# One load ahead of four crossbar transposes, a score tile for the last rows of x, and full-array steps in front of the AV runs, in a fused attention and GELU kernel

## The chip, the cores and the metric

One core of one Trainium2 chip. The metric is the device time of one execution in microseconds (us). The kernel before takes 350.77 us (median of three runs, 350.18 to 350.9). Granted TensorE clocks are given as shares of full speed. A run is called slow when it is over 1.5% above the fastest of the same kernel; ratios use the other runs, the fast ones. A kernel counts as faster or slower from 2% on; no verdict here reaches that (part 3 alone is once "unclear", all others are "same"), so the arguments rest on the traces. Three chips served for the experiments, and each experiment is compared with runs of the kernel before on its own chip.

## The reference, cut to what matters

Causal attention with a forget gate for 8 batches x 8 heads x 576 tokens x 64, then a two-layer GELU network on the 4608 rows that come out.

```python
q, k, v: (8, 8, 576, 64)   f: (8, 8, 576)   w_in: (512, 2048)   w_out: (2048, 512)
cum    = cumsum(log(clip(f, 1e-4, 1)))
scores = q @ k.T / 8 + cum[:, :, :, None] - cum[:, :, None, :]     # causal
x      = softmax(scores) @ v                                       # -> (4608, 512)
out    = gelu(x @ w_in) @ w_out
```

## The kernel before: the parts that matter

The kernel works batch by batch. In a batch, TensorE makes the scores of four head pairs, each in four tiles; ScalarE takes the exponentials; GpSimd masks the diagonal blocks; TensorE multiplies with v (an "AV run": two heads, 30 products); VectorE normalizes the rows, which are transposed into xT. Then the first product (`gemm1`, 16 blocks of 4 products with w_in) runs alone. The second product of the previous batch fills the gaps of the attention, a few steps at a time.

q and k of batch b come in through GpSimd's queue, which also turns them to bf16, are transposed by the crossbar from SyncE's queue, and are untangled by VectorE during the first product of batch b-1. v comes in on SyncE's queue too, and GpSimd multiplies it with the forget weights ("weighs" it). v has one buffer, so its load waits for the weighing of the batch before. Batch 1 has a layout of its own:

```python
def load_v(b, h0=0, h1=H):                    # five loads on SyncE's queue
    for n in range(NBLK):
        nc.sync.dma_start(v_sb[...], v[b, ...])

def transpose_dma(b, h0, h1):                 # one q and one k transpose, SyncE's queue
    for src, dst in zip(qk_of[b], tq_of[b]):
        nc.sync.dma_start_transpose(dst[...], src[...])

def untangle(b, i):                           # VectorE: 4 copies for q, 4 for k (L242)
    ...
def weigh_v(b, i, eng=nc.gpsimd):             # L258: vw = v * w, a head pair at a time
    ...
def second_attention():                       # batch 1
    ...
    for i in range(HP):
        for t in range(4):
            scores(b, i, t)
            ...
            if (i, t) == (3, 0):
                transpose_dma(2, 0, 4)
                transpose_dma(2, 4, 8)
    ...
    gemm1_begin(1, both)
    x_tail(1)
    load_v(2)                                 # behind the transposes

for b in range(B):
    ...
    for ffb in range(0 if b > 1 else 4, n_ff):
        gemm1(b, ffb)                         # 16 blocks; 12 of them for batch 1
        ...
        if b == 1 and ffb == 4:
            load_qk_tokens(3)                 # GpSimd's queue; q,k have two buffers
        first, gap = (5, 3) if b == 1 else (0, 4)
        at, late = divmod(ffb - first, gap)
        if late == 0:
            untangle(b + 1, at)
        if late == gap - 2:
            weigh_v(b + 1, at)
        if ffb == 14 and b > 1:
            load_qk_tokens(b + 2)
```

The second product takes row steps ("r": two products on 64 rows each, side by side into two PSUM banks) or full-array steps ("n": one product on 128 rows into one bank):

```python
PLAN = [                                      # block of rows, banks, steps
    (0, "o", 16 * "r"),
    (1, "m", 15 * "r" + "n"),
    (2, "m", 16 * "r"),
    (3, "s", 8 * "r" + 8 * "n"),
]
```

PSUM has two banks each under the names "o" (AV results) and "m" (products), and two double tiles "s" (scores). The transpose of x through TensorE takes an "o" bank.

The softmax here doesn't subtract the row's maximum and nothing guards it: scores larger than these inputs give would overflow.

## Time and profile before

| | before |
|---|---|
| time, median of 3 | 350.77 us |
| profiled span | 348.6 us, TensorE busy 96% |
| first AV run of batch 2, with the full step ahead of it | 84.26 to 87.00 us |
| the next AV run, with its step | 90.97 to 92.30 us |
| first crossbar-transposed k of batch 2 copied from | 62.94 us |
| length of a batch from batch 3 on | 36.3 us |

The instants are read from the timelines of single engines, in us from the start of the profiled span: a line there gives start, length, engine, source line, operation, operands, count, and in brackets the idle time just before it with what ended it. The lines themselves stand in the prediction.

### The profile page before, as it was taken

To read this page: it belongs to the slowest core of one execution; us is meant where nothing else is said; L and a number is where in the kernel's file an instruction comes from. 1 tells how busy PE (TensorE), PEld (TensorE's weight loads), DVE (VectorE), ACT (ScalarE), POOL (GpSimd) and SP (SyncE) were. 2 spreads that over 40 slices of the span, in tenths; PEclk is the share of its full clock that TensorE was granted. 3 is DMA by queue.
4 is the path that set the end of the run, shared out by engine and by line. 5 is a ranking of instruction groups with operands and counts; after the bars stand their busy time and mean duration, and the time that the engine had idled before them with its cause. 6 is when DMAs were issued, how large, how long until landed. Compare 5 with 4: busy or idle time off the path is not lost.

```text
span 348.6 us, 7941 instructions
## 1 busy us (share of the span) xinstructions
PE 334.8 (96%) x3211; PEld 175.9 (50%) x3242; DVE 188.0 (54%) x424; ACT 212.8 (61%) x296; POOL 124.0 (36%) x256
## 2 busy tenths in 40 slices
PE   8899999998989999999999999999999999999995
PEld 3674555444554455545654465446544554444443
DVE  4770456853366934796469746975498452011011
ACT  5976786772643687468746874687567764603600
POOL 8480872109328034443436243714270430000000
PEclk9999999999999999999999999999999999999999
DMA  7999999992990999268944997398900130011013
GB/s 117 177 190 194 196 197 193 174 188 80 215 199 30 137 187 185 83 87 159 202 121 73 132 233 139 55 159 199 176 32 0 52 100 30 2 60 60 2 30 91
DMA packets 99924, 43.03 MB, mean 123 GB/s; under 512 B 78704, under 2 KB 95344, under 8 KB 99888
## 3 DMA queue, kind: packets, MB, share of 16 engines
q1 hardware_dynamic: 82592, 28.37, 41.1%
q0 software_dynamic: 16896, 13.63, 26.3%
q8 instruction: 25, 0.41, 0.5%
q10 hardware_dynamic: 400, 0.52, 0.4%
q14 instruction: 11, 0.09, 0.1%
HBM read 36.85 MB, written 9.44 MB: 133 GB/s over the span
## 4 chain that ended last, share of the span: by engine, by line
PE 68%; DMA 10%; SPq 10%; ACT 4%; POOL 4%; issue 2%; DVE 0%; POOLq 0%; ACTq 0%; DVEq 0%
PE ps L370 28%; PE ps L461 20%; PE ps L403 8%; PE o L318 7%; SPq L117 7%; DMA v_sb<-in_v_dram 6%; PE s L287 5%; DMA k<-in_k_dram 3%; SPq L228 3%; POOL vw L258 2%; ACT e L297 2%; ACT L297 2%; ACT g L387 1%; PE ps_x L348 1%; POOL q L105 1%
## 5 line engine op out<-in xcount | busy, mean ns | idle before, releaser
L387 ACT ACTIVATE g<-ps 128x512 bf16<-128x512 f32 x144 | 85.3, 597 | 81.8 <-PE ps L370 81.8
L297 ACT ACTIVATE e<-s 128x896 bf16<-128x896 f32 (+2 forms) x128 | 101.6, 837 | 32.6 <-PE s L287 30.9
L370 PE MATMUL ps<-xT,w_in_sb 128*128 128x512 bf16 x502 | 111.6, 379 | 0.5
L461 PE MATMUL ps<-w_out_sb,g 64*128 64x512 bf16 (+1 forms) x756 | 102.7, 376 | 1.1 <-issue 0.8
L370 PEld LDWEIGHTS <-w_in_sb 128*128 128x128 bf16 x576 | 55.9, 98 | 67.5 <-issue 1.8
L299 POOL TENSOR_SCALAR_AFFINE_SELECT e<-e 128x256 bf16<-128x256 bf16 (+1 forms) x135 | 49.2, 383 | 101.4 <-ACT e L297 101.1
L461 PEld LDWEIGHTS <-g 64*128 64x128 bf16 (+1 forms) x771 | 41.7, 94 | 36.2 <-issue 5.5
L242 DVE COPY qT<-tq 64x288 bf16<-64x288 bf16 x96 | 49.1, 511 | 1.7 <-DMA tq<-q 0.3
L287 PE MATMUL s<-qT,kT 64*128 64x320 bf16 (+4 forms) x384 | 46.0, 277 | 4.0 <-ACT e L297 2.6
L258 POOL TENSOR_TENSOR vw<-v_sb,wT 128x640 bf16<-128x640 f32 x31 | 39.7, 1281 | 22.3 <-DMA v_sb<-in_v_dram 22.2
L318 PE MATMUL o<-vw,e 128*128 128x65 bf16 x960 | 37.5, 194 | 2.7 <-issue 0.8
L469 DVE COPY ot<-ps 128x512 f32<-128x512 f32 x26 | 17.9, 690 | 40.7 <-PE ps L461 36.5
L318 PEld LDWEIGHTS <-e 128*128 128x128 bf16 x960 | 33.6, 98 | 12.1 <-issue 7.3
L242 DVE COPY kT<-tk 64x288 bf16<-64x288 bf16 x96 | 32.6, 340 | 2.8 <-DMA tk<-k 1.2
L332 DVE TENSOR_TENSOR x<-o,r 128x320 bf16<-128x320 f32 x64 | 31.5, 492 | 2.4 <-DVE r L331 0.2
L287 PEld LDWEIGHTS <-kT 64*128 64x128 bf16 x384 | 20.2, 94 | 24.8 <-issue 11.7
L412 DVE COPY ot<-ps 128x512 f32<-128x512 f32 (+2 forms) x9 | 5.7, 633 | 48.8 <-PE ps L403 48.8
L403 PE MATMUL ps<-w_out_sb,g 128*128 128x512 bf16 (+2 forms) x142 | 27.9, 355 | 0.1
L331 DVE RECIPROCAL r<-o 128x5 f32<-128x5 f32 x64 | 12.2, 190 | 27.6 <-PE o L318 27.4
L403 PEld LDWEIGHTS <-g 128*128 128x128 bf16 x144 | 13.5, 98 | 14.5
L471 DVE TENSOR_TENSOR ot<-ot,ps 128x512 f32<-128x512 f32 x26 | 17.9, 688 | 1.5
L360 POOL COPY tails<-xT 128x256 bf16<-128x256 bf16 x8 | 3.2, 396 | 31.9 <-DVE xT L351 31.9
(64 smaller groups left out, 160.1 us busy)
## 6 DMA issues: line engine op xcount, KB each, us to landing
out_dram<-ot SPq DMA_DIRECT2D x32, 256.0 KB, 2.3
v_sb<-in_v_dram SPq DMA_DIRECT2D x24, 256.0 KB, 4.9
q<-in_q_dram POOLq DMA_DIRECT2D x6, 576.0 KB, 6.3
k<-in_k_dram POOLq DMA_DIRECT2D x6, 576.0 KB, 8.5
v_sb<-in_v_dram SPq DMA_DIRECT2D x22, 128.0 KB, 5.6
w_in_sb<-in_moe_w_in_dram POOLq DMA_DIRECT2D x4, 512.0 KB, 6.8
w_out_sb<-in_moe_w_out_dram POOLq DMA_DIRECT2D x4, 512.0 KB, 11.9
q<-in_q_dram POOLq DMA_DIRECT2D x4, 144.0 KB, 4.5
```

What stands on the lines that cost most here:

```text
L117: nc.sync.dma_start(v_sb[p0:P, h0:h1, n, :], v[b, h0:h1, K0[n] + p0 : K0[n] + P].rearrange("h p d -> p h d"),)
L242: nc.vector.tensor_copy(rows[:, odd], src[odd * D : (odd + 1) * D, 2 * i + h].rearrange("d j p -> d p j"),)
L258: eng.tensor_tensor(vw_of[b][:, hs, :, 0:D], v_sb[:, hs, :, :], w.unsqueeze(3).to_broadcast([P, 2, NBLK, D]), Alu.mult,)
L287: nc.tensor.matmul(to, *ab, start=half < 0, stop=half == 1 or not masked)
L297: nc.scalar.activation(et[:, :, z:c], st[:, :, z:c], Act.Exp, scale=scale)
L299: nc.gpsimd.affine_select(out=et[:, :, c0 + z : c0 + P], in_=et[:, :, c0 + z : c0 + P], compare_op=Alu.is_ge, fill=0.0, base=z, pattern=[[ ...
L318: nc.tensor.matmul(o[:, m, :], e_of[b, i, t][:, h, c : c + P], vw_of[b][:, 2 * i + h, n, :], start=(n == 0), stop=(n == m),)
L332: nc.vector.tensor_tensor(x_of[b, i][:, :, h, :], o[:, :, 0:D], r.unsqueeze(2).to_broadcast([P, NBLK, D]), Alu.mult,)
L370: nc.tensor.matmul(ps, w_in_sb[:, kt, ffb * P : (ffb + 1) * P], src[:, kt, 0:TC], start=(kt == 0), stop=(kt == n_dm - 1),)
L387: nc.scalar.activation(g_of[c][ffb], ps, Act.Gelu)
L403: nc.tensor.matmul(pss[ts][:, c0:c1], g_of[c][kt][:, ts * P : (ts + 1) * P], w_out_sb[:, kt, c0:c1], start=(kt == 0), stop=(kt == n_ff - 1),)
L461: nc.tensor.matmul(banks[r], g_of[c][kt][rows, ts * P : (ts + 1) * P], w_out_sb[rows, kt, :], start=(kt == 0), stop=last if r else kt == n ...
```

## The change

The intent was to take away three small idle times of TensorE. (1) Wherever an AV run follows row steps, a full-array step is put between them, since a switch from half-array to full-array products costs a little time. (2) The transpose of the last rows of x but one in batch 2 goes through a score tile, so that the last AV run needn't wait for an "o" bank. (3) v of batch 2 is queued ahead of the crossbar transposes of batch 2's q,k, so that it is weighed, and the masks are made, before the first AV run of batch 2 needs them.

```diff
 def to_xT(b, i, copy, pool=m_psum, tag="m", ps=None):
     if ps is None:
-        ps = pool.tile([P, XC], BF16, tag=tag, name="ps_x")
+        shape = [P, 2, 1024] if pool is s_psum else [P, XC]
+        ps = pool.tile(shape, BF16, tag=tag, name="ps_x")
+        if pool is s_psum:
+            ps = ps[:, 0, 0:XC]
 ...
 PLAN = [
     (0, "o", 16 * "r"),
-    (1, "m", 15 * "r" + "n"),
-    (2, "m", 16 * "r"),
-    (3, "s", 8 * "r" + 8 * "n"),
+    (1, "m", 5 * "r" + "n" + 9 * "r" + "n"),
+    (2, "m", 9 * "r" + "n" + 6 * "r"),
+    (3, "s", 7 * "r" + 9 * "n"),
 ]
 ...
 if b == 2:
-    to_xT(b, HP - 2, nc.vector.tensor_copy, o_psum, "o")
+    to_xT(b, HP - 2, nc.vector.tensor_copy, s_psum, "s")
 ...
+if (i, t) == (2, 0):
+    load_v(2)
 if (i, t) == (3, 0):
     transpose_dma(2, 0, 4)
     transpose_dma(2, 4, 8)
 ...
 x_tail(1)
-load_v(2)
```

## The prediction

> **What bounds the kernel now.** I read the page first, then the chain of waits, then the timelines of the engines where the chain leaves TensorE.
>
> ```profile
> span 348.6 us, 7941 instructions
> PE 334.8 (96%) x3211; PEld 175.9 (50%) x3242; DVE 188.0 (54%) x424; ACT 212.8 (61%) x296; POOL 124.0 (36%) x256
> ```
>
> TensorE is busy 334.8 of 348.6 us and no other engine is over 61%. A change can only pay where it fills TensorE's 13.8 us of idle time or shortens the stream itself. The chain of waits (start, length, what) leaves TensorE for long between 41 and 86 us:
>
> ```profile
> 41.52 12.04 DMA k<-in_k_dram
> 53.57 4.04 SPq L228
> 57.66 2.72 SPq L228
> 60.43 2.31 SPq L228
> ...
> 66.38 12.21 DMA v_sb<-in_v_dram
> 78.75 1.28 POOL vw L258
> ...
> 84.33 1.66 POOL e L299 x5
> 86.04 0.97 PE o L318 x25
> ```
>
> So: q,k of batch 2 land, SyncE issues their four crossbar transposes (L228), then the load of v; v lands at 78.6 us; GpSimd weighs it (L258), and only then masks the exponentials (L299) that the first AV run of batch 2 (the products with v, L318) waits for. TensorE's timeline shows what that costs, against the next AV run, which waits for nothing:
>
> ```profile
> 84.26 0.38 PE L461 MATMUL ps<-w_out_sb,g 128*128 128x512 bf16 x1 [0.16 <-issue]
> 84.72 0.23 PE L318 MATMUL o<-vw,e 128*128 128x65 bf16 x2
> 85.68 1.32 PE L318 MATMUL o<-vw,e 128*128 128x65 bf16 x28 [0.73 <-POOL e L299]
> ...
> 90.97 0.38 PE L461 MATMUL ps<-w_out_sb,g 128*128 128x512 bf16 x1 [0.16 <-issue]
> 91.19 1.11 PE L318 MATMUL o<-vw,e 128*128 128x65 bf16 x30
> ...
> 101.70 0.64 PE L318 MATMUL o<-vw,e 128*128 128x65 bf16 x15
> 103.03 0.64 PE L318 MATMUL o<-vw,e 128*128 128x65 bf16 x15 [0.69 <-DVE xT L351]
> ```
>
> The first run takes 84.26 to 87.00 (85.68+1.32), that is 2.74 us; the second 90.97 to 92.30, 1.33 us. Loss: 1.41 us. The last run is cut in two, because its second head needs the o bank that the transpose of x just filled and VectorE has not emptied: 103.03 - 101.70 = 1.33 us from head to head where about 0.46 (half a run's pace) is enough. Loss: about 0.87 us.
>
> VectorE then shows how batch 2's q,k are unpacked (L242, "untangled") during the first product of batch 1:
>
> ```profile
> 60.40 1.34 DVE L242 COPY qT<-tq 64x288 bf16<-64x288 bf16 x4 [0.32 <-DMA tq<-q]
> 62.94 1.36 DVE L242 COPY kT<-tk 64x288 bf16<-64x288 bf16 x4 [1.20 <-DMA tk<-k]
> ...
> 71.76 1.34 DVE L242 COPY kT<-tk 64x288 bf16<-64x288 bf16 x4
> 74.77 0.69 DVE L507 TENSOR_TENSOR ot<-ot,ps 128x512 f32<-128x512 f32 x1 [1.67 <-PE ps L496]
> ```
>
> The first transposed q landed at about 60.4, the first k at 62.9, and the eight groups of four copies (q and k of four head pairs) end at 73.1. TensorE's scores of batch 2 start at 72.53. This slack is what the change spends.
>
> **What the Trainium skill says.** "DMA: Bandwidth & Descriptors", section "Queues, rings and completion order": each DMA engine takes turns between the queue rows that have work, a packet at a time, and descriptors of one row are consumed in ring order. The packet records agree: from 68 to 74 us, with q,k of batch 3 (packets of 768 B, GpSimd's queue) beside v (256 B, SyncE's queue), both move about 180 to 200 packets per us; v alone at 86 to 90 moves about 950 per us, the transposes alone at 94 to 98 about 800. So a GpSimd load cuts the SyncE queue to a quarter. "TensorEngine Tiling (Array Packing)", section "Key Properties": "Mode switching requires drain". The trace agrees, and it is cheap: about 0.12 us per switch, below. "TensorE: Matmul & The Clock Gate", section on the array's architectural detail: VectorE's queue is strictly first in, first out; so the two additions of L507 cannot pass untangling copies that are issued before them. In this trace they never do.
>
> **The change, part by part.**
> 1. *Full-array step in front of AV.* A step is either two 64-row products into two banks, side by side, or one 128-row product. Both cost about 0.216 us from start to start. In the steady batches of before, one AV run already has the full step in front, and the others don't:
>
> ```profile
> 163.22 1.04 PE L461 MATMUL ps<-w_out_sb,g 64*128 64x512 bf16 x8
> 164.20 1.12 PE L318 MATMUL o<-vw,e 128*128 128x65 bf16 x30
> ...
> 167.44 0.82 PE L461 MATMUL ps<-w_out_sb,g 64*128 64x512 bf16 x6
> 168.43 1.11 PE L318 MATMUL o<-vw,e 128*128 128x65 bf16 x30 [0.16 <-issue]
> ```
>
> Without it: four row steps, 4 x 0.216 = 0.86, from 163.22 give 164.08; AV starts at 164.20, 0.12 late. With it (its record is missing, but its weight load is there): three row steps and one full, also 0.86, from 167.44 give 168.30; AV starts at 168.43, 0.13 late. The drain is paid ahead of the full step instead of ahead of AV. AV itself is 0.01 shorter. Net 0.00 us for each of 3 runs x 5 batches; I allow 0.2 either way.
> 2. *The last rows of x through a score tile.* Removes the 0.87 us wait. But the transpose of the last x (105.00) comes 6 steps later and needs VectorE to have normalized both heads: 103.93+0.49 = 104.42 now, about 104.26 with the second head right behind the first. TensorE would be there at about 104.15, so it starts at about 104.4 instead of 105.0. Gain 0.6 us.
> 3. *v ahead of the transposes.* v's load then waits only for the weighing of batch 1, done at 46.7, so its packets start at about 48 instead of 64. v is weighed and masks are written in time: gain 1.41 us. What it pushes back: v has 4608 packets. Beside q,k and w_out on GpSimd's queue (still about 1040 packets of 768 B at 185 per us and 1024 of 1024 B at 155: 5.6+6.6 us, so to about 60.3), v moves about 2100; the other 2500 at 1000 per us end at about 62.7. The transposes stand behind them in the ring.
> The built program adds something that the diff doesn't show. In before, the pool gives q,k of batch 3 the buffer of batch 2, so that their load waits for the transposes (issued at 64.31, the first q and k transposes long landed). In the changed build they get batch 1's buffer, and wait for TensorE's old reads only. GpSimd can issue them at 60.6; with the 2.5 us to first packets seen in before they run from about 63.0 to 71.5 (1536 at 180). The transposes meet them from the start: some 300 packets alone, 8.5 x 180 = 1530 beside them, then 750 per us. The first q and k need 2304, reached at 72.1; in before landing came 1 to 2 us after the count. So the first k lands at about 73.5, not 62.9.
> From there VectorE has all groups but the first q's to copy, 7 x 1.35 = 9.45, then two L507 of 0.69, with 0.1 of signals: the banks of the second product are free at 73.5+10.9 = 84.4. TensorE wants them at its 49th step after 72.53, at 80.75. Delay 3.7 us: about 2.4 of it before the first scores (73.5+1.45 against 72.53), the rest at that bank.
> Sum: -0.0 -0.6 -1.4 +3.7 = +1.7 us, 352.4.
>
> **The rivals.** (a) The transposes are fast enough: if the first k lands before 80.75-10.95 = 69.8, nothing of the 3.7 is paid and the time is 350.8-2.0 = 348.8. For it: v is finished at about 62, and alone a transpose takes some 1.6 us. Against it: under a GpSimd load the first one needed from 54 to 60.4. (b) Part paid: landing near 71.5 makes 1.7 us of delay and a tie, 350.5. (c) Landing at 75 or later, a long idle of TensorE and perhaps a lower clock after it: 354 or more. The clock row shows no loss after short idles in before. (d) A true gain from part 1, if the weight loads of AV hide behind the full step: at most the 0.01 us per run seen, 0.2 in all.
>
> **Range and chances.** I give the sum with a late transpose 65%, rival (a) 25%, the rest to ties; weighted, 351.3. The range 348.7 to 353.8 holds all but (c). Two per cent is 7.0 us, and no part comes near it: faster 0.01, slower 0.02.
>
> **What would show it.** VectorE's timeline: first kT<-tk copy of batch 2 near 73.5 (theory) or under 69.8 (rival a); the first scores of batch 2 after a wait on VectorE; the first L461 step on the m banks waiting for L507. GpSimd's issue of q for batch 3 near 60.6. The first AV run of batch 2 unbroken, 1.33 us with its full step; the last one unbroken. AV runs of later batches 0.12 us behind a row step, as before; batch length still 36.3 us (164.20 to the next batch's 200.5). If later batches change in length, part 1 is misjudged; if the first k lands early, my packet rates are.

## The result, and the profile after

The changed kernel takes 353.15 us (median of four: 352.74, 352.71, 353.56 and a slow one of 359.14); the kernel before, in the same rounds, 350.75. The ratio is 1.0067 (95%: 1.0045 to 1.0089): a little slower, within 2%. Ratios here are the mean time of one kernel's fast runs over that of the other's fast runs of the same rounds, so not quite the ratio of the medians quoted.

Two lines of the page of the changed kernel:

```profile
span 350.7 us, 7898 instructions
PE 332.4 (95%) x3182; PEld 175.5 (50%) x3227; DVE 187.7 (54%) x424; ACT 212.7 (61%) x296; POOL 124.9 (36%) x256
```

The span is 2.1 us longer. The number of TensorE instructions is no measure of the work here: some matmul records are missing from each trace. The weight loads (PEld), 15 fewer, fit the plan: each of 3 added full steps, in 5 batches, loads one weight tile where a row step loads two.

GpSimd's timeline of the changed kernel: the load of q of batch 3, and the first weighing of v of batch 2.

```profile
60.74 0.84 POOL L105 DMA_DIRECT2D q<-in_q_dram  x1
...
64.47 1.28 POOL L258 TENSOR_TENSOR vw<-v_sb,wT 128x640 bf16<-128x640 f32 x1 [2.12 <-PE ps L373]
```

The load of batch 3's q is issued at 60.74 (64.31 before; 60.6 was predicted), because it no longer waits for the transposes. The weighing begins at 64.47 instead of 78.75. That was what the reordering is for.

The chain of waits of the changed kernel (start, length, what), where it leaves v's load for the transposes:

```profile
58.09 3.26 SPq L117
...
61.39 10.75 DMA tq<-q
```

SyncE finishes issuing v (L117) at 61.35, and the first transpose is issued at 61.39 and lands 10.75 us later, at 72.14. The packet records, counted per microsecond, say why: SyncE's queue moved nothing from 63.81, where v's last packet started, to 66.23, while GpSimd's load moved 250 to 265 packets per us alone; from 67 to 70 the transposes moved 185 to 189 per us, as many as that load (184 to 190); from 70 on, with the load ending (last packet at 71.12), 424 to 1120. The first k landed at 73.09.

VectorE's timeline of the changed kernel from there on:

```profile
72.16 1.34 DVE L242 COPY qT<-tq 64x288 bf16<-64x288 bf16 x4 [12.01 <-DMA tq<-q]
73.52 1.35 DVE L242 COPY kT<-tk 64x288 bf16<-64x288 bf16 x4
...
82.03 1.49 DVE L242 COPY kT<-tk 64x288 bf16<-64x288 bf16 x4
83.55 1.29 DVE L510 TENSOR_TENSOR ot<-ot,ps 128x512 f32<-128x512 f32 x2
```

The eight groups of copies run from 72.16 to 83.52 instead of 60.40 to 73.10. The additions (L510; L507 before) that empty the two "m" banks of the second product stand behind them and end at 84.84.

TensorE's timeline. First three lines of before that the prediction doesn't show: the first scores of batch 2, the first eight products after them, and the first step into the "m" banks.

```profile
72.53 0.37 PE L287 MATMUL s<-qT,kT 64*128 64x256 bf16 x4
72.83 1.90 PE L496 MATMUL ps<-w_out_sb,g 128*128 128x512 bf16 x8
...
80.75 1.89 PE L461 MATMUL ps<-w_out_sb,g 64*128 64x512 bf16 x16
```

The same stretch in the changed kernel, then the first and the last AV run of batch 2, and one AV run of a later batch:

```profile
74.23 0.28 PE L287 MATMUL s<-qT,kT 64*128 64x256 bf16 x1 [1.56 <-DVE kT L242]
74.93 0.36 PE L287 MATMUL s<-qT,kT 64*128 64x256 bf16 x3 [0.41 <-DVE kT L242]
75.22 1.90 PE L499 MATMUL ps<-w_out_sb,g 128*128 128x512 bf16 x8
...
84.29 0.37 PE L464 MATMUL ps<-w_out_sb,g 64*128 64x512 bf16 x1 [0.99 <-DVE ot L510]
84.89 1.88 PE L464 MATMUL ps<-w_out_sb,g 64*128 64x512 bf16 x15 [0.23 <-DVE ot L510]
...
88.39 0.38 PE L464 MATMUL ps<-w_out_sb,g 128*128 128x512 bf16 x1 [0.16 <-issue]
88.61 1.11 PE L318 MATMUL o<-vw,e 128*128 128x65 bf16 x30
...
104.42 1.11 PE L318 MATMUL o<-vw,e 128*128 128x65 bf16 x30
...
165.24 0.82 PE L464 MATMUL ps<-w_out_sb,g 64*128 64x512 bf16 x6
166.22 1.11 PE L318 MATMUL o<-vw,e 128*128 128x65 bf16 x30 [0.16 <-issue]
```

Both AV runs that were broken are now whole, the first at 88.61 and the last at 104.42 (30 products in 1.11 us each). In exchange TensorE waits in two new places: 1.56 + 0.41 us for the untangled k, and 0.99 + 0.23 us for a bank that VectorE empties late. The account, from instants of these two timelines (start to start):

| stretch | before | after | difference |
|---|---|---|---|
| start of the span to the first AV run of all | 17.38 | 17.45 | +0.07 |
| from there to the full step ahead of batch 2's first AV run (84.26; 88.39) | 66.88 | 70.94 | +4.06 |
| from that step to the next AV run's step (90.97; 93.69) | 6.71 | 5.30 | -1.41 |
| from the second AV run (91.19; 93.91) to batch 3's first (127.90; 129.92) | 36.71 | 36.01 | -0.70 |
| sum up to batch 3 | | | +2.02 |
| batches 3 to 6 (to the first AV run of batch 7) | 145.18 | 145.20 | +0.02 |

The +4.06 and the offset of 0.07 make 4.13, and split so: the first scores come 1.70 later (72.53 to 74.23), the eight products after them another 0.69 later, the first step into the banks another 1.15, and from that step to the full step another 0.59.

### The profile page after: what moved, and what is told of

It is laid out like the page before. It is cut to its first block, busy times and chain, and to the rows that moved or that the text cites. A ratio compares the mean times of both kernels' runs of the same rounds, so it can differ in the third digit from the quotient of the medians.

```text
span 350.7 us, 7898 instructions
## 1 busy us (share of the span) xinstructions
PE 332.4 (95%) x3182; PEld 175.5 (50%) x3227; DVE 187.7 (54%) x424; ACT 212.7 (61%) x296; POOL 124.9 (36%) x256
## 4 chain that ended last, share of the span: by engine, by line
PE 67%; SPq 10%; DMA 6%; ACT 5%; DVE 4%; POOL 4%; issue 3%; POOLq 0%; ACTq 0%; DVEq 0%
PE ps L373 28%; PE ps L464 19%; SPq L117 10%; PE ps L406 8%; PE o L318 7%; PE s L287 5%; DMA tq<-q 3%; DMA v_sb<-in_v_dram 3%; ACT e L297 3%; ACT L297 2%; DVE qT L242 2%; POOL vw L258 1%; DVE kT L242 1%; ACT g L390 1%; PE ps_x L351 1%
## 5 line engine op out<-in xcount | busy, mean ns | idle before, releaser
L464 PE MATMUL ps<-w_out_sb,g 64*128 64x512 bf16 (+1 forms) x731 | 100.9, 376 | 2.0 <-DVE ot L510 1.2
L299 POOL TENSOR_SCALAR_AFFINE_SELECT e<-e 128x256 bf16<-128x256 bf16 (+1 forms) x135 | 50.0, 387 | 117.9 <-ACT e L297 117.5
L318 PEld LDWEIGHTS <-e 128*128 128x128 bf16 x960 | 34.8, 98 | 5.3 <-PE ps_x L351 0.3
L474 DVE TENSOR_TENSOR ot<-ot,ps 128x512 f32<-128x512 f32 x26 | 17.9, 687 | 1.5
L373 PE MATMUL ps<-tails,w_in_sb 128*128 128x512 bf16 x63 | 14.3, 377 | 0.1
```

The lines of the kernel that those rows point to most:

```text
L299: nc.gpsimd.affine_select(out=et[:, :, c0 + z : c0 + P], in_=et[:, :, c0 + z : c0 + P], compare_op=Alu.is_ge, fill=0.0, base=z, pattern=[[ ...
L318: nc.tensor.matmul(o[:, m, :], e_of[b, i, t][:, h, c : c + P], vw_of[b][:, 2 * i + h, n, :], start=(n == 0), stop=(n == m),)
L373: nc.tensor.matmul(ps, w_in_sb[:, kt, ffb * P : (ffb + 1) * P], src[:, kt, 0:TC], start=(kt == 0), stop=(kt == n_dm - 1),)
L464: nc.tensor.matmul(banks[r], g_of[c][kt][rows, ts * P : (ts + 1) * P], w_out_sb[rows, kt, :], start=(kt == 0), stop=last if r else kt == n ...
```

## The experiments

**The theory at this point:** parts 1 and 2 do what was predicted; part 3's loss comes from the load of batch 3's q,k, which lost its wait and slows the transposes of batch 2. **Rivals:** v ahead of the transposes is by itself too late for them, whatever the load does; or part 1 costs time, hidden by gains elsewhere.

### Each part alone (one chip; the kernel before there: 350.98, 349.16 to 354.12, 11 runs)

The first kernel has the three lines of `PLAN` alone:

> Before with part 1 alone (full-array step in front of three more AV runs of each of five batches). Theory (a mode switch costs about 0.12 us wherever it falls): same time as before, within 0.2 us, and the batches stay 36.3 us long. Rival (the full step hides the first weight loads of AV, or the switch was dearer in front of AV): 15 runs gain 0.1 us each, 1.5 us faster.

Measured: 351.44 us (349.86 to 354.3), ratio 1.0019 (0.997 to 1.0067). The times can't settle tenths. The trace can: first AV runs of batches 3, 4 and 5 at 128.78, 165.08 and 201.37, so 36.30 a batch, against 36.29 before. Part 1 is worth nothing, and costs nothing: the drain of a switch is paid ahead of the full step instead of ahead of AV.

The second has the edit of `to_xT` and its score tile alone:

> Before with part 2 alone (last rows of x of batch 2 through a score tile). Theory: the last AV run of batch 2 is unbroken and the transpose of the last x starts 0.6 us earlier, total 0.6 us faster. Rival (VectorE's queue sets the second transpose anyway): under 0.2 us.

Measured: 350.13 us (348.77 to 353.03), ratio 0.9985 (0.9935 to 1.0034). In its trace the last AV run of batch 2 is whole, and the second AV run to batch 3's first takes 36.00 us (92.58 to 128.58) instead of 36.71. Part 2 gains 0.71.

The third has the move of `load_v(2)` alone:

> Before with part 3 alone (v of batch 2 ahead of the transposes; its build also gives q,k of batch 3 the buffer of batch 1). Theory: this part alone holds the whole loss: the changed kernel's +2.1 us of span and the 0.6 us that part 2 gives back, so about 2.7 us slower than before, first k copy of batch 2 near 73.5 us, VectorE done with the copies and the two additions near 84.8. Rival (the loss comes from an interplay of the three parts): under 1.5 us slower.

Measured: 357.3 us (354.45 to 358.17), ratio 1.0165 (1.0113 to 1.0216; unclear, since the interval reaches past 2%). A miss by more than 3 us. The trace shows a thing that the changed kernel's doesn't: v's last load landed only at 71.7 instead of 64.2, so v was weighed from 72.02 to 77.86, right beside the first untangling copies. The first q group took 3.61 us instead of 1.34, TensorE sat idle 4.42 us before the first scores, and the eight products after them took 3.56 us instead of 1.90.

### Does part 3 do this only when alone? The changed kernel and part 3 again (a third chip; before there: 352.36, 349.88 to 355.94, 11 runs)

Both kernels unchanged, on one chip. The changed kernel:

> The changed kernel again, beside the others on one chip. Theory: its time is not one number but depends on how long TensorE waits for the first k of batch 2: near 353 where the last load of v got ahead of q,k of batch 3, and 356 to 359 where it did not, because v is then weighed beside the copies and TensorE's wait grows past 4 us and its clock drops. So a spread of over 3 us between runs, with granted clocks of 0.99 in the long ones. Rival (the long run seen at first was chance): all runs within 1 us of 353.

Measured: 356.41 us (355.4 to 357.39, and one run at 352.33), ratio 1.0089 (1.0028 to 1.0151; the kernel before is slower and more spread on this chip). Part 3 alone again:

> Part 3 alone again. Theory: it has the same spread as the changed kernel, plus 0.6 us; on one chip the two differ by 0.6 us or by which of the two cases a run falls in. Rival (parts 1 and 2 protect the changed kernel): part 3 alone always longer by 3 us or more.

Measured: 356.8 us (355.3 to 357.75), ratio 1.0113 (1.006 to 1.0166), and the same pattern in its trace. So it is no property of part 3 alone: the changed kernel has two ways to run. Its trace here, first on GpSimd and VectorE:

```profile
71.65 1.28 POOL L258 TENSOR_TENSOR vw<-v_sb,wT 128x640 bf16<-128x640 f32 x1 [9.37 <-PE ps L373]
...
73.10 4.64 DVE L242 COPY qT<-tq 64x288 bf16<-64x288 bf16 x4 [13.01 <-DMA tq<-q]
```

And on TensorE:

```profile
78.47 0.39 PE L287 MATMUL s<-qT,kT 64*128 64x256 bf16 x1 [5.87 <-DVE kT L242]
...
79.65 3.45 PE L499 MATMUL ps<-w_out_sb,g 128*128 128x512 bf16 x8
```

Compare line by line with the changed kernel's first trace. On GpSimd the weighing starts at 71.65, not 64.47, as v's fifth load landed only at 71.35 (the profile puts the wait down to a product on TensorE, which was long done). The issue of that load ended at 63.02 here and at 61.35 there, while the load of batch 3's q was issued at the same time (60.68 and 60.74). With 1.7 us less of a head start v's last packets fell under GpSimd's load and came out 7 us later: SyncE's queue pauses here too, from 64.56 to 66.52, and only 4096 of v's 4608 packets, four of its five loads, had gone before the pause; in the first trace all 4608 had. Both traces of part 3 alone show the late case (4096 before a pause). That the head start decides is read from these four traces; no run moved it alone. The first copies fall beside the weighing and take 4.64 us. TensorE's idle time before the scores is 5.87 us, and the eight products after it take 3.45 us.

The windows of this trace (stretch, its length, busy time and instructions of TensorE, its weight loads, VectorE, ScalarE and GpSimd, then granted clock, DMA share, GB/s) show why the products are slow:

```profile
79.00:84.00 5.00, 4.83 (x19) 1.63 (x20) 4.76 (x15) 2.73 (x3) 0.85 (x2) 0.62 0.00 0
```

The clock is 0.62 after the idle time; in the changed kernel's first trace, after 1.56 + 0.41 us of idle, the same window has 1.00. The Trainium skill, "TensorE: Matmul & The Clock Gate", section "What's actually happening", gives half clock after an idle window of about 3.4 us. The idle time of 5.87 us agrees: it began at 72.61, and the granted clock was 1.00 up to 76.0 and 0.50 from there to 82.8. That of 4.42 us, in part 3 alone, agrees less well: it began at 74.43, and the clock was 0.50 from 76.6 on, 2.2 us into it. These runs still count as fast, for they are compared with their own fastest run; the mean clock of 0.99 marks them. The slow run of 359.14 in the first result has a clock of 0.99 too, but no trace, so its cause isn't shown.

### Taking the load of batch 3 out of the way

Three experiments take the load away from the transposes. First, the changed kernel with q,k of batch 3 asked for behind the weighing (on the chip of the single parts):

```diff
-if b == 1 and ffb == 4:
-    load_qk_tokens(3)
 ...
-if ffb == 14 and b > 1:
+if ffb == (15 if b == 1 else 14):
     load_qk_tokens(b + 2)
```

> The changed kernel, but q,k of batch 3 are asked for behind the four weighings of batch 2 instead of ahead of them. v still stands ahead of the transposes. Theory (the load of q,k of batch 3 beside the transposes is what delays them): the load goes out near 70 us, the transposes run alone from about 64 us, the first k copy of batch 2 starts near 67.5, before 69.8, no TensorE wait at the first scores; about 348.8 us, 2.0 faster than before and 4.2 faster than the changed kernel. Rival (v ahead in the same ring is enough to delay them): first k near 70 or later and 350.5 or more.

Measured: 350.46 us (349.58 to 352.57), ratio 0.9991 (0.9947 to 1.0035). The first half of the theory holds: without the load beside them SyncE's queue has no pause, and the first q and k landed at 65.92 and 67.57. The gain didn't come, since the copies still ended late, at 81.47 instead of 83.52, and the wait at the bank stayed (0.99 + 0.22 us). The answer for the tile qT (count: shortest, median and longest duration in ns, first and last start, form) and GpSimd's timeline of this kernel:

```profile
L242 DVE COPY qT<-tq x4: 681/1445/1452, 65.9 to 69.6; 64x288 bf16<-64x288 bf16 x4
```

```profile
66.62 1.27 POOL L258 TENSOR_TENSOR vw<-v_sb,wT 128x640 bf16<-128x640 f32 x1
...
68.09 1.27 POOL L258 TENSOR_TENSOR vw<-v_sb,wT 128x640 bf16<-128x640 f32 x1
```

A copy that takes about 0.33 us otherwise takes 1.445, and GpSimd's period is 68.09 - 66.62 = 1.47 us. While GpSimd weighs, VectorE gets one copy through per weighing. The Trainium skill, "SBUF — State Buffer", section "Who interferes with whom", calls the pair of ports that the two engines share an exclusive lock: the engine that comes second is blocked for the whole instruction of the first, not slowed down. The numbers agree.

Second, the changed kernel with fixed buffers, so that q,k of batch 3 go to batch 2's buffer and wait for the transposes, as in the kernel before (on a second chip; before there: 352.12, 349.8 to 354.53, 11 runs):

```diff
-qk_pool = ...tile_pool(name="qk", bufs=2)
+qk_pool = ...tile_pool(name="qk", bufs=1)
-    qk_pool.tile([PT, H, JT * D], BF16, tag=n, name=f"{n}{b}")
+    qk_pool.tile([PT, H, JT * D], BF16, tag=f"{n}{(b + (b > 2)) % 2}", name=f"{n}{b}")
```

> The changed kernel with one thing undone by hand: q,k of batch 3 get the buffer of batch 2 again, as before's build had it, so that their load waits for the transposes; nothing moves in the program. Theory (the lost wait is the cause): the load goes out near 69 us, the first k copy of batch 2 starts near 67.5, no TensorE wait at the first scores, 348.8 us. Rival (v ahead of the transposes is enough): as the changed kernel, 352 or more.

Measured: 355.72 us (353.41 to 356.64), ratio 1.009 (1.0038 to 1.0142). Again the transposes are early (first copies of q and k at 65.96 and 67.50) and the first scores on time (72.56). But the load waits for the transposes on GpSimd, in order, and the weighing stands behind it: 72.14 to 78.10. The third q group beside it took 5.73 us, the copies ended at 82.72, TensorE waited 2.55 us at the bank, and then the clock fell, as the windows of this trace show:

```profile
84.00:87.00 3.00, 2.91 (x14) 1.15 (x15) 1.33 (x3) 0.00 (x0) 0.00 (x0) 0.50 0.86 249
```

Third, what settles whether v ahead of the transposes is too late by itself: the first of these three kernels, with GpSimd's weighing held until VectorE has copied the last k (a tiny GpSimd copy reads it). Run on the third chip:

```diff
-if late == gap - 2:
+if late == gap - 2 and b > 1:
     weigh_v(b + 1, at)
+if b == 1 and ffb == 15:
+    done = x_pool.tile([P, 1], BF16, tag="done", name="done")
+    nc.gpsimd.tensor_copy(done, kT[3][:, S - 1 : S])
+    for pair in range(HP):
+        weigh_v(2, pair)
```

> The changed kernel with q,k of batch 3 asked for late (as in the run before it of that kind), and the four weighings of batch 2 held back until VectorE has copied the last k. Theory (GpSimd's weighing beside the copies was what cost the 4 us there, 5.06 instead of 1.34 for the first group): all eight groups take 1.34 to 1.6, first k copy near 67.5, copies done near 77, the additions near 78.2, no wait at TensorE's bank; v weighed from 77 to 82.5, first AV run of batch 2 waits under 0.5 us; 348.8 to 349.4 us. Rival (v ahead of the transposes is itself too late): copies end after 80, 350.5 or more.

Measured: 352.12 us (351.76 to 353.3), ratio 0.9991 (0.9936 to 1.0046). The total misses, but the point in question is answered on VectorE's timeline:

```profile
68.72 1.36 DVE L242 COPY kT<-tk 64x288 bf16<-64x288 bf16 x4 [0.31 <-DMA tk<-k]
```

All eight groups take 1.34 to 1.36 us, the copies end at 78.29, and TensorE waits for VectorE neither at the first scores nor at the bank. So v ahead of the transposes isn't too late by itself; the load beside the transposes and the weighing beside the copies are what cost. The total misses because the time is only handed on: weighing ends at 84.2, masks at 88.4, and the first AV run of batch 2 is broken again (1.03 + 0.71 us of waits). The profile puts the first of these waits down to an addition of VectorE (L474) that ended at 86.18, but the first mask ended at that time too, and in the changed kernel the run starts before that addition ends (88.61 against 89.76). Later comes a wait of 0.89 us for a transpose of x, on a SyncE queue that runs late: v of batch 3, now beside the late load, lands at 99.11 instead of 92.95.

### The other order

The kernel before, with q,k of batch 3 in batch 1's buffer (the tag becomes `f"{n}{b % 2}"`), so that the load comes early while the transposes still stand ahead of v, on the second chip:

> Before with q,k of batch 3 in batch 1's buffer, so that their load no longer waits for the transposes (it goes out near 60.6 us instead of 64.3); v stays behind the transposes. Theory (the lost wait costs only when the transposes still stand behind v): the first q and k have landed by 63, only the last two transposes meet the load, the copies still end before 80; v lands between 76 and 79, so the first AV run still waits up to 1.4 us; 350.0 to 350.8, as before. Rival (the early load is harmful by itself): over 1.5 us slower than before.

Measured: 349.96 us (349.61 to 350.96), ratio 0.9931 (0.9887 to 0.9976). An early load does no harm there. Its trace is not a clean comparison, with everything up to batch 2 about 1.7 us later than in the trace of before (first scores of batch 2 at 74.22). In batch 0 TensorE waits 0.54 us for k there, and its granted clock is 0.50 from 17.1 to 20.5. Its first AV run of batch 2 is whole, for which that delay may be needed.

Last, a version meant to beat both: the kernel before with part 2, and the load of batch 3 behind the weighing as in the first of the three above. The transposes stay ahead of v. On the second chip:

> Before with part 2, and q,k of batch 3 asked for behind the weighings of batch 2; v stays behind the transposes. If the contention of that load with whatever stands on SyncE's queue is the cause on both sides, v moves alone from 64 us and lands near 70 instead of 78.6, the first AV run of batch 2 is unbroken (gain 1.4), the copies are as in before, part 2 gives 0.6: about 348.8 us without part 3. Rival (v lands late for its place in the ring): the AV wait stays, 350.2.

Measured: 348.68 us (347.88 to 348.97), ratio 0.9887 (0.9843 to 0.9931), as expected. Once more on the third chip:

> Transposes ahead of v, q,k of batch 3 asked for behind the weighings, x through a score tile: a repeat on another chip or at another hour. Theory: 348.7 again, 2 us faster than a before that is not disturbed (350.7), and little spread, since nothing on TensorE's path then depends on a race of two loads. Rival: its lead of 1.1 per cent was due to a slow before, under 0.2 per cent here.

Measured: 348.39 us (348.31 to 349.07), ratio 0.9883 (0.9835 to 0.9932). VectorE and then TensorE in this trace:

```profile
71.20 5.67 DVE L242 COPY kT<-tk 64x288 bf16<-64x288 bf16 x4
```

```profile
84.30 1.11 PE L318 MATMUL o<-vw,e 128*128 128x65 bf16 x30
```

Without the load beside it v lands in time to be weighed from 70.99 on (78.75 before), early enough for the masks and a whole AV run. The weighing still blocks one group (5.67 us), but it is the last, with slack behind it: the two additions end at 78.2, and TensorE takes the banks at 80.58. This is the best version, 2.1 to 2.4 us under an undisturbed run of before (350.75). The larger ratio of 1.2% is partly due to the kernel before, which spreads from 350 to 356 us on those two chips. The granted clocks point to the reason: its ten runs of 353.3 us or more on the three chips show 0.990 to 0.995, the other 23 show 0.997 to 1.0, and the trace with q,k of batch 3 in batch 1's buffer, at 0.994, has one stretch at half clock in batch 0. That the long runs of before have the same isn't shown, for no trace of one was taken.

## Why the prediction was right, and where it was not

The time, 351.3, is the sum of the parts (352.4) weighted with rivals. The result of 353.15 lies in the range, and within 2%. Step by step:

- **Full steps, 0.00: right.** Batches keep 36.30 us, in the changed kernel and in the part alone; AV still starts 0.12 us late, at 166.22, where six row products and the full step from 165.24 make 165.24 + 4 x 0.216 = 166.10.
- **Score tile, -0.6: right**, measured -0.70 in the whole and -0.71 alone.
- **Whole first AV run, -1.41: right**, measured -1.41.
- **The delay, +3.7: right in mechanism, mis-sized by 0.36** (measured 4.06). The term that was off is the copying: seven groups were put at 7 x 1.35 = 9.45, and took 83.52 - 73.52 = 10.00, as three of them needed 1.44 to 1.55. Beside each of these GpSimd wrote masks (from 77.66, 80.61 and 82.25); in the kernel with the held weighing no mask ran beside the copies, and none needed more than 1.36. The banks came free at 84.84 instead of 84.4. The part before the first products was put at 2.4 and measured 75.22 - 72.83 = 2.39.
- **The first k at 73.5: 73.09 landed, 73.52 copied, but by luck, as two errors cancelled.** The transposes did not meet the load "from the start" at 180 packets per us: nothing moved on their queue from 63.8 to 66.2, and up to 1120 per us moved at the end. The first q, which the sum took as copied already when k lands, landed only at 72.14.
- **Rival (a), an early landing: fell.** It came true only where the load was taken away (first k landed at 67.57), and even there the gain was not kept.
- **Rival (c), a long idle and a lower clock, left outside the range: it exists.** It did not decide the first result, but five of six runs of the changed kernel on the third chip took 355.4 to 357.4. The step behind it that failed was the even flow of v: that v ends "at about 62.7" was taken as settled, when it is a race of v's last load with GpSimd's. And the sum didn't know that weighing and untangling exclude each other: from a late v follow late copies, though the transposes land nearly on time (73.10 for the first q copy instead of 72.16).
- **Slips that moved nothing much.** Half an AV run's pace is 0.52 us, not 0.46 (91.19 to the next instruction at 92.23, halved). The row step at 80.75 is the 33rd step after 72.53; it is the 49th product. From GpSimd's issue to its load's first packet before shows 2.0 us (64.31 to 66.28), not 2.5.

So the load that lost its wait was found in the built program ahead of the run, and is about half of the story: with it moved away, the first AV run of batch 2 starts 86.56 - 17.22 = 69.34 us after the first of all, against 88.61 - 17.45 = 71.16 in the changed kernel, and 67.10 would be no delay at all (84.26 + 0.22 for the full step, less 17.38), so 2.24 of the 4.06 remain. What was missed is that v and the transposed q,k meet a second time, as weighing and untangling, on GpSimd and VectorE.

## What to carry to other kernels

Before a load is moved ahead in a queue, work out who is now behind it and what else may start earlier in the built program: here a buffer pool gave the next load another buffer, and with it took a wait away that had kept two transfers apart. Where long pieces of GpSimd and VectorE block each other, as weighing and untangling do here, plan them into different stretches, or let the blocked piece be one with slack behind it. A median near the prediction may be one of two ways to run: run it on another chip and look at the trace before the sum is believed.

## What the Trainium skill lacked or had wrong

- "TensorE: Matmul & The Clock Gate", section "What's actually happening": an idle window of about 3.4 us isn't needed to lose the clock. An idle time of 2.55 us at a bank, one product, and 0.18 us more were followed by a clock of 0.50 for the next 3 us (15 products in 3.36 us instead of 1.88). With q,k of batch 3 in batch 1's buffer, the clock was 0.50 from 17.1 to 20.5 after waits of at most 0.54 us; TensorE had been busy 2.00 of the 3.41 us before, with small products. Idle times of 1.56 + 0.41 us were not followed by it (1.00). Where the line runs, these traces don't say.
- "SBUF — State Buffer", section "Who interferes with whom": right on the lock, but it doesn't say what a run of GpSimd instructions does. VectorE got one copy in for each weighing, 1.445 us a copy instead of 0.33, so that four weighings held one group of four copies for 3.6 to 5.7 us instead of 1.34.
- "DMA: Bandwidth & Descriptors", section "Queues, rings and completion order": taking turns by packet is stated and agrees (185 to 189 packets per us on SyncE's queue beside 184 to 190 of GpSimd's casting load; up to 1120 without it). It has no word on a pause when such a load gets going: SyncE's queue moved nothing for 1.9 to 2.6 us in all five traces where the load was asked for early, with v's last load or transposes waiting on it. No such pause stands in the three traces of the changed kernel with the load moved away, where the transposes follow v at once. In the kernel before, where v meets the load, SyncE's queue falls to 30 packets in one us. The cause of the pause isn't shown.
- "TensorEngine Tiling (Array Packing)", section "Key Properties": the drain at a switch has no figure there. Here it is about 0.12 us, and it is the same whether an AV run or a full step of the second product comes after row steps.
